# Two transformer layers on one core: part by part reordering of the sequence stage, of the y turn and of the weight preparation

## The chip, the cores and the metric

One core of a Trainium2 chip runs the whole program in one launch. The metric is the device time in microseconds (us); three runs of the kernel before took 2637.14, 2634.07 and 2632.92 us, median 2634.07.

## The reference

Input x is 2048 x 576 (S x D) in fp32. Two layers, each a Fourier mixing and an MLP:

```
A(x) = Cr @ (x @ dr.T) - Ci @ (x @ di.T)         # 2048 x 2048 and 576 x 576 DFT matrices
B(x) = gelu(layernorm(x) @ w1 + b1) @ w2 + b2    # 576 -> 4608 -> 576
for layer in range(2):
    x = x + A(layernorm(x))
    x = x + B(layernorm(x))                       # both layers use the same weights
```

## The kernel before, in words

**Products of parts.** TensorE gets each fp32 operand as two rounded parts: ACT copies it to a high part (fp32r), VectorE subtracts to make the low part. A product is three matmul passes, (high, high), (high, low), (low, high), in PASSES as (left, right). The large products go by a scheme with seven block products in place of eight (numbered 1 to 7, in the order ORDER); it needs sums and differences of blocks on both sides, which VectorE and POOL make, and its results are combined in PSUM and SBUF.

**Sequence stage** (class Sequence). S x S times S x 576, from x that has been normalized, in NT = 16 row tiles of output. The right operand is 8 pairs of x tiles, Z[p], each with 7 blocks in two parts: three plain blocks (rows 0 to 2 of Z), b12 aside, and four sums (rows 3 to 6). While the pairs come in, the first PLAIN = 2 tiles are made by eight plain products (`first_mms(p)`, 48 matmuls per pair, banks 0 to 7), so that TensorE has work. A generator, `fill`, emits for every pair: loads, statistics (`norm_stats`), mean and scale by a pow on POOL, `normalize` on ACT, high parts (`high_left`, `high_z`), low parts (`low_left`, `low_z`), and the sums (`right_sums` on VectorE and POOL, `high_sums`, `low_sums`). `run` emits first_mms(p) as soon as pair p's emission is done. Then come 14 tiles of seven products of 24 matmuls (`mms`), each with left blocks loaded (`load_c`), summed (`sums`), cut in parts (`high` three steps ahead, `low` two steps ahead) and results collected (`post`). BANK gives each product its bank; products that share one are accumulated or follow each other. In layer 1 the first pairs are prepared inside the MLP before (early = True).

**Weight preparation.** w1 is cut in parts once, in layer 0: `weights()` is a generator of 4 + 1 + 2 x 126 steps (18 column pairs q of 7 blocks), driven by `pump()`. Of each two steps one emits the low part of block n (VectorE), the sum that follows it (POOL) and the high part of block n + 1 (ACT), the other the store of block n to DRAM and perhaps a load for the next q. Three stage slots hold the parts: block n + 3 reuses block n's. `made[0]` is q + 1 once pair q's seven blocks are stored. In the sequence stage of layer 0 two pumps follow each product but product 2 (L759 to 761). In the first MLP `advance` pumps at the places in BEHIND, twelve per group from group 1 on, and `load_w` has `while made[0] <= q: pump()` ahead of a load of pair q's parts. Five slots hold loaded w1 parts there, so the first block of q + 1 is asked for before the fourth product of q.

**Hidden stage and MLP.** `hidden` multiplies with the 576 x 576 matrices, normalizes, and turns blocks of 128 tokens (index j) by TensorE into y, seven rows of blocks with two parts. `turn_y(3)` does so for the last block, between the first products of the MLP (`inner(0, 0)`, first half of the tokens, columns 0 to 255 of y; the second half follows). `parts(2, ...)` makes the parts of block 2. In `mlp`, `inner(q)` makes seven products into banks 0 to 3 or 4 to 7 and their gelu, `outer(g, i, side)` multiplies by w2. The list `due` holds the steps that make w2's parts in the first MLP (`make(g)`), by place within the group. Each engine executes in the order in which its instructions are emitted.

Of the kernel before, what the change touches and what calls it, by code (L numbers as in the profile page):

```python
# [15 lines left out]
P = 128  # L16
# [17 lines left out]
ORDER = (1, 6, 2, 5, 7, 3, 4)  # L34
BANK = {1: 0, 2: 0, 6: 1, 5: 2, 3: 2, 7: 3, 4: 3}
# [10 lines left out]
PASSES = ((0, 0), (0, 1), (1, 0))  # L46

# [111 lines left out]
def spectral_mixer(ctx: ExitStack, tc: tile.TileContext, x, dh, c0, cs, w1, b1, w2, b2, out):  # L159
# [102 lines left out]
    def weights():  # L262
# [5 lines left out]
                 (7, a21, None), (6, a11, None), (3, a12, None))  # L268
# [25 lines left out]
        def keep(n):  # L294
# [3 lines left out]
            if k in (2, 4, 5, 6):  # L298
                load(q + 1, (2, 4, 5, 6).index(k))
# [28 lines left out]
    class Sequence:  # L328
        def __init__(self, src, early):
# [4 lines left out]
            self.normal, self.begun, self.xs, self.before = set(), {}, [], self.prepare()  # L334
            self.pieces = self.fill()
# [33 lines left out]
        def fill(self):  # L369
# [32 lines left out]
            else:  # L402
# [14 lines left out]
                self.high_parts(0)  # L417
                yield
            for p in range(NP):
# [22 lines left out]
                if p == 0 and not self.early:  # L442
                    self.half_stats(1)
                    self.low_z(0)
                    self.norm_stats(1)
                    self.low_left(0)
                    yield
# [39 lines left out]
            self.low(*self.steps[0], True)  # L487
            self.high(*self.steps[1])
            self.right_sums(NP - 1)
            self.high(*self.steps[2])  # L490
            self.high_sums(NP - 1)
            self.low(*self.steps[1])
# [44 lines left out]
        def norm_stats(self, p):  # L537
            if p not in self.mv:
# [3 lines left out]
                self.mv[p] = stats_of_pair(st, mv, p == 0 and not self.early, p > 2, p == 1 and not self.early)  # L542

        def normalize(self, p):
            for h in range(2):
                at = slice(2 * h, 2 * h + 2)
                if p == 0 and not self.early:
                    v, mv = self.x[p][:, at], self.mv[p][:, h]
                    nc.vector.tensor_scalar(v, v, mv[:, 0:1], mv[:, 3:4], op0=OP.subtract, op1=OP.mult)
                    continue  # L550
                if p == 1 and not self.early:
                    shift(self.mv[p][:, h])
# [27 lines left out]
        def low_left(self, p):  # L580
            c = self.left(p)
            sub(nc.vector, c[:, 1], self.lv[p], c[:, 0].bitcast(F32))
# [21 lines left out]
        def first_mms(self, p):  # L604
            c, z, b = self.left(p), self.Z[p](7, 2, DH), self.b12[p](2, DH)
            right = {(1, 1): z[:, 0], (2, 2): z[:, 1], (2, 1): z[:, 2], (1, 2): b}
            cells = [(t, i, j, k) for t in range(PLAIN) for i in (1, 2) for j in (1, 2) for k in (1, 2)]
            steps = [(*cell, n) for n in range(3) for cell in cells]
            if p == NP - 1:
                steps = [(*cell, n) for cell in cells for n in range(3)]  # L610
            for t, i, j, k, n in steps:
                o, (u, w) = banks[4 * (1 - t) + 2 * (i - 1) + j - 1][:, :DH], PASSES[n]
# [56 lines left out]
        def low(self, t, i, sums=False):  # L669
            v = self.cells[t, i](2, NP, P)  # L670
            sub(nc.vector, v[:, 1], self.source(t, i), v[:, 0].bitcast(F32))
            if sums:
                self.sums(t)
# [798 lines left out]
```

## Time and profile before

| what | value |
|---|---|
| median of three runs | 2634.07 us |
| profiled execution, own time | 2634.11 us |
| its span, first to last instruction | 2632.3 us |
| TensorE matmul (PE), weight loads (PEld) busy | 2617.2 us, 2466.4 us |
| VectorE (DVE), ScalarE (ACT), GpSimd (POOL) busy | 1834.1, 1118.3, 796.7 us |
| granted TensorE clock | 1.000 |

Busy times are unions over the span. A matmul's end is modelled, and matmuls overlap. SP issues most transfers. The helpers at L196 (add), L199 (subtract), L202 (split) and L209 (matmul) record many operations under one line. The sequence stage of layer 0 takes the first 380 us or so, its first MLP lies at about 450 to 850 us, layer 1's sequence stage begins near 1319 us.

### The profile page before, as it was taken

How to read it: one execution, taken by the hardware profiler on the slowest of the kernel's cores; microseconds unless marked ns; L12 is line 12 of the kernel's file. 1: busy time of each engine (PE TensorE's matmuls, PEld its weight loads, DVE VectorE, ACT ScalarE, POOL GpSimd, SP SyncE). 2: the span in 40 equal slices, each digit the busy share in tenths (PEclk: the TensorE clock that was granted, in tenths of full speed). 3: DMA queues.
4: the chain of work that ended last, by engine and by line, in shares of the span. 5: the costliest groups of instructions: out<-in, count | busy, mean ns of one | idle time of the engine just before them, and what ended most of it. 6: DMA issues, size and time to landing. Idle time of an engine off the chain costs nothing. (4 is left out here: it accounts for less than half of the span.)

```text
span 2632.3 us, 44772 instructions
## 1 busy us (share of the span) xinstructions
PE 2617.2 (99%) x17252; PEld 2466.4 (94%) x17252; DVE 1834.1 (70%) x2574; ACT 1118.3 (42%) x1815; POOL 796.7 (30%) x644
## 2 busy tenths in 40 slices
PE   9999999999999999999999999999999999999999
PEld 9999999899999989998999999999999999899998
DVE  8999987878777665556687776576555557655555
ACT  6555555555453443333354333353333325433332
POOL 6333433534444332222251000132222233322222
PEclk9999999999999999999999999999999999999999
DMA  5687786788788666677554333746666685666664
GB/s 184 226 273 241 244 259 215 262 276 286 275 286 299 184 194 195 195 222 212 170 177 132 124 123 124 210 153 192 195 195 195 195 274 157 200 195 194 194 195 156
DMA packets 223238, 544.91 MB, mean 207 GB/s; under 512 B 23712, under 2 KB 74912, under 8 KB 222880
## 3 DMA queue, kind: packets, MB, share of 16 engines
q1 hardware_dynamic: 209632, 511.94, 61.9%
q10 hardware_dynamic: 13392, 30.09, 3.0%
q8 instruction: 137, 2.24, 0.3%
q14 instruction: 77, 0.63, 0.1%
HBM read 429.87 MB, written 114.72 MB: 207 GB/s over the span
## 5 line engine op out<-in xcount | busy, mean ns | idle before, releaser
L209 PE MATMUL bank<-R 128*128 128x288 f32 (+2 forms) x16972 | 2587.4, 315 | 9.0 <-DVE R L199 3.8
L209 PEld LDWEIGHTS bank<-R 128*128 128x128 f32 x16972 | 2435.4, 189 | 157.0 <-DVE R L199 7.0
L196 DVE TENSOR_TENSOR A<-bank,A 128x576 f32<-128x576 f32 (+3 forms) x810 | 567.5, 708 | 520.2 <-PE bank L209 464.2
L199 POOL TENSOR_TENSOR R<-A,R 128x512 fp32r<-128x512 f32 (+1 forms) x290 | 376.0, 1305 | 909.6 <-ACT R L1261 548.7
L199 DVE TENSOR_TENSOR R<-A,R 128x1024 fp32r<-128x1024 f32 (+9 forms) x535 | 530.4, 1017 | 43.8 <-ACT R L667 12.5
L1261 ACT ACTIVATE R<-A 128x512 fp32r<-128x512 f32 x288 | 177.5, 630 | 355.7 <-DVE A L199 222.1
L196 POOL TENSOR_TENSOR A<-A 128x576 f32<-128x576 f32 (+2 forms) x102 | 156.2, 1536 | 539.5 <-ACT A L708 344.2
L1200 ACT ACTIVATE bank<-bank,b1t 128x512 f32<-128x512 f32 (+1 forms) x224 | 144.9, 647 | 360.9 <-DVE bank L196 235.8
L199 POOL TENSOR_TENSOR A<-A 128x288 f32<-128x288 f32 (+3 forms) x152 | 192.6, 1271 | 200.1 <-DVE R L199 95.3
L196 DVE TENSOR_TENSOR bank<-bank,A 128x512 f32<-128x512 f32 (+1 forms) x228 | 152.2, 669 | 143.5 <-PE bank L209 142.6
L667 ACT ACTIVATE R<-A 128x1024 fp32r<-128x1024 f32 x196 | 206.1, 1053 | 103.4 <-PE bank L209 60.2
L199 DVE TENSOR_TENSOR A<-A 128x1024 f32<-128x1024 f32 (+3 forms) x166 | 164.5, 996 | 6.2
L199 DVE TENSOR_TENSOR R<-bank,R 128x512 fp32r<-128x512 f32 x232 | 156.2, 676 | 4.3 <-ACT R L1261 3.7
L1261 ACT ACTIVATE R<-bank 128x512 fp32r<-128x512 f32 x216 | 121.1, 595 | 32.5 <-PE bank L209 32.5
L199 DVE TENSOR_TENSOR A<-bank,A 128x512 f32<-128x512 f32 x144 | 98.1, 681 | 0.4
L1227 ACT ACTIVATE A<-bank 128x512 f32<-128x512 f32 (+1 forms) x76 | 43.7, 575 | 120.2 <-PE bank L209 120.2
L282 ACT ACTIVATE R<-A 128x256 fp32r<-128x256 f32 x126 | 51.9, 412 | 64.0 <-DMA w_parts<-R 23.1
L1200 ACT ACTIVATE A<-bank,b1t 128x512 f32<-128x512 f32 (+1 forms) x76 | 50.5, 665 | 66.6 <-DVE bank L196 66.5
L230 POOL TENSOR_TENSOR moments<-moments,power 128x1 f32<-128x1 f32 x32 | 26.7, 834 | 129.8 <-DVE moments L232 112.0
L283 ACT ACTIVATE R<-A,power,middle 128x128 fp32r<-128x128 f32 x126 | 60.6, 481 | 0.0
L256 ACT ACTIVATE A<-A,moments 128x576 f32<-128x576 f32 x58 | 49.0, 866 | 23.5 <-POOL moments L252 13.6
L1135 ACT ACTIVATE R<-A 128x576 fp32r<-128x576 f32 x63 | 42.2, 676 | 15.8 <-DVE A L199 7.2
(65 smaller groups left out, 609.6 us busy)
## 6 DMA issues: line engine op xcount, KB each, us to landing
R<-w_parts SPq DMA_DIRECT2D x504, 320.0 KB, 3.4
R<-w_parts SPq DMA_DIRECT2D x189, 576.0 KB, 3.7
A<-in_cs SPq DMA_DIRECT2D x112, 512.0 KB, 4.5
w_parts<-R SPq DMA_DIRECT2D x63, 576.0 KB, 5.1
w_parts<-R ACTq DMA_DIRECT2D x81, 320.0 KB, 3.8
uv_mid<-A SPq DMA_DIRECT2D x28, 576.0 KB, 5.4
w_parts<-R SPq DMA_DIRECT2D x45, 320.0 KB, 4.5
A<-in_w SPq DMA_DIRECT2D x72, 192.0 KB, 4.9
```

What stands on the lines that cost most here:

```text
L196: engine.tensor_tensor(dst, a, b, op=op)
L199: engine.tensor_tensor(dst, a, b, op=OP.subtract)
L209: nc.tensor.matmul(o, a, b, start=start, stop=stop, skip_group_check=True)
L230: nc.gpsimd.tensor_tensor(mv[:, 3:4], mv[:, 2:3], power[:, 0:1], op=OP.pow)
L256: nc.scalar.activation(dst, src, AF.Identity, bias=mv[:, 4:5], scale=mv[:, 3:4])
L282: nc.scalar.activation(t[:, 1:4:2], src[:, 0:3:2], AF.Copy)
L283: nc.scalar.activation(t[:, 2], src[:, 1], AF.Identity, bias=power[:, 2:3], scale=middle)
L667: nc.scalar.activation(self.cells[t, i](2, NP, P)[:, 0], self.source(t, i), AF.Copy)
L1135: nc.scalar.activation(got2[g, i](2, 2, DH)[:, :, 0], src, AF.Copy)
L1200: nc.scalar.activation(dst, src, AF.Gelu_apprx_tanh, bias=bias(f))
L1227: nc.scalar.activation(up, o, AF.Copy)
L1261: nc.scalar.activation(H[q, k](2, TC)[:, 0], src, AF.Copy)
```

## The change

It has these parts; the core of the diff follows.

- First pairs, layer 0: `first_parts` makes the parts of pair 0 in halves on ACT; the left low parts of pair 0 come in two halves around the statistics of pair 1, and the right low parts after them. Pair 7 gets its mean and scale by VectorE and ACT (`quick`), no longer by POOL.
- `first_mms` passes in the order (high, high), (low, high), (high, low), and with other orders of cells; in the last pair all (high, high) first.
- The first seven-product tile runs in the order FIRST; product 2 has a bank of its own there, and is added by VectorE. The emission at the end of `fill` is ordered for it.
- No pump in the first seven products, and none after the third product of a tile; the preparation's blocks 6 and 7 are exchanged, with the loads that follow.
- `turn_y`: the seven short transposes go to other banks, four and three apart; the low parts of block 2 come after the whole turn.
- MLP: places of w2's steps in the first and the last group; one difference on POOL for the first q.

```diff
+FIRST = (1, 2, 6, 5, 7, 3, 4)
+LEFT_FIRST = ((0, 0), (1, 0), (0, 1))
 # weights()
-                 (7, a21, None), (6, a11, None), (3, a12, None))
+                 (6, a11, None), (7, a21, None), (3, a12, None))
-                load(q + 1, (2, 4, 5, 6).index(k))
+                load(q + 1, {2: 0, 4: 2, 5: 1, 6: 3}[k])
 # Sequence
+            self.quick = (NP - 1,) if early else (1, NP - 1)
-                self.high_parts(0)
+                self.first_parts()
                 if p == 0 and not self.early:
+                    self.low_left(0, 0)
                     self.half_stats(1)
+                    self.norm_stats(1)
+                    self.low_left(0, 1)
                     self.low_z(0)
-                    self.norm_stats(1)
-                    self.low_left(0)
-            self.low(*self.steps[0], True)
+            self.right_sums(NP - 1)
             self.high(*self.steps[1])
-            self.right_sums(NP - 1)
+            self.low(*self.steps[0])
+            self.low(*self.steps[1])
+            self.sums(PLAIN)
+            sub(nc.vector, self.block(PLAIN, 0), self.tmp(NP, P), self.block(PLAIN, 0))
+            self.high_sums(NP - 1)
             self.high(*self.steps[2])
-            self.high_sums(NP - 1)
-            self.low(*self.steps[1])
             self.low_sums(NP - 1)
...
-                self.mv[p] = stats_of_pair(st, mv, p == 0 and not self.early, p > 2, p == 1 and not self.early)
+                self.mv[p] = stats_of_pair(st, mv, p == 0 and not self.early, 2 < p < NP - 1, p in self.quick)
+        def first_parts(self):
+            x, z, mv = self.x[0], self.Z[0](7, 2, DH), self.mv[0]
+            self.parts[0], self.b12[0] = self.own.take(), self.b12s[0]
+            left = self.left(0)
+            for h in range(2):
+                v = x[:, 2 * h:2 * h + 2]
+                nc.vector.tensor_scalar(v, v, mv[:, h, 0:1], mv[:, h, 3:4], op0=OP.subtract, op1=OP.mult)
+            nc.scalar.activation(left[:, 0, 0:4], self.lv[0][:, 0:4], AF.Copy)
+            nc.scalar.activation(z[:, 0, 0], x[:, 1], AF.Copy)
+            nc.scalar.activation(self.b12[0](2, DH)[:, 0], x[:, 0], AF.Copy)
+            nc.scalar.activation(z[:, 1:3, 0], x[:, 2:4], AF.Copy)
+            nc.scalar.activation(left[:, 0, 4:8], self.lv[0][:, 4:8], AF.Copy)
 # first_mms
+            if p == 0:
+                cells = [(t, i, j, k) for t in range(PLAIN) for k in (1, 2) for j in (1, 2) for i in (1, 2)]
+            elif p < NP - 1:
+                cells = [(t, i, j, k) for j in (1, 2) for t in range(PLAIN) for i in (1, 2) for k in (1, 2)]
             steps = [(*cell, n) for n in range(3) for cell in cells]
             if p == NP - 1:
-                steps = [(*cell, n) for cell in cells for n in range(3)]
+                steps = [(*cell, 0) for cell in cells] + [(*cell, n) for cell in cells for n in (1, 2)]
 # begin_loads, low, mms, post
-            self.steps = [(t, i) for t in range(PLAIN, NT) for i in ORDER]
+            self.steps = [(t, i) for t in range(PLAIN, NT) for i in (ORDER if t > PLAIN else FIRST)]
-            if i == 2:
+            if i == (2 if t > PLAIN else 6):
                 sub(nc.vector, self.block(t, 1), self.block(t, 1), self.block(t, 0))
+        def bank(self, t, i):
+            return banks[4 - 4 * (t % 2) + (3 if t == PLAIN and i == 2 else BANK[i])][:, :DH]
+            elif i == 2 and t == PLAIN:
+                add(nc.vector, uv[:, 0, 1], b, p1)
 # run
-                if i != 2:
+                if n % 7 != 2 and n >= 7:
                     pump()
                     pump()
 # turn_y, hidden
-            o = space()
-            for i0 in (0, 4):
+            late = space()[:, 1:2, :3 * P]
+            for i0, o in ((0, pp[0][:, :, TC // 2:]), (4, late)):
...
-        for n in (4, 2, 0):
+        for n in (4, 1, 1):
             next(mlp)
             for m in range(n):
-                if n == 4 and m == 2:
-                    parts(2, slice(0, 4), slice(3, 7), high=False, engine=nc.gpsimd)
-                    t8s.give(t8.pop(2))
                 next(y_steps)
+        parts(2, slice(0, 4), slice(3, 7), high=False, engine=nc.gpsimd)
+        t8s.give(t8.pop(2))
 # mlp
-                return (list(zip((22, 23, 26), one + five[:1])),
-                        list(zip((6, 6, 8, 8, 10, 10, 12, 12, 14, 14, 16), five[1:] + six + three + seven + two + four)))
+                return (list(zip((22, 25), one)),
+                        list(zip((6, 7, 7, 8, 8, 10, 10, 12, 12, 14, 14, 16), five + six + three + seven + two + four)))
-                    sub(nc.vector if n < 4 or first and q == 0 and n < 6 else nc.gpsimd, h[:, 1], src, h[:, 0].bitcast(F32))
+                    sub(nc.vector if n < 4 or first and q == 0 and n == 5 else nc.gpsimd, h[:, 1], src, h[:, 0].bitcast(F32))
-                due.extend((n, step) for n, (_, step) in zip((3, 4, 5, 6, 9, 10), soon + late[:4]))
+                due.extend((n, step) for n, (_, step) in zip((3, 4, 7, 8, 11, 12), soon + late[:4]))
```

## Rows read from the trace of the kernel before

**Rows 1.** Page, first part: busy us (share of the span) xinstructions.
```profile
PE 2617.2 (99%) x17252; PEld 2466.4 (94%) x17252; DVE 1834.1 (70%) x2574; ACT 1118.3 (42%) x1815; POOL 796.7 (30%) x644
```
**Rows 2.** Waits of the weight loads, whole span: us in total, times, longest us.
```profile
PEld bank L209 <- DVE R L199: 7.0, 13, 1.5
```
**Rows 3.** Timeline, first pairs: start, us, engine, line, operation [idle before <-releaser].
```profile
8.91 1.43 DVE L199 TENSOR_TENSOR R<-A,R 128x864 fp32r<-128x864 f32 x2 [0.43 <-ACT R L569]
...
11.60 1.68 POOL L247 TENSOR_TENSOR moments<-moments,power 128x2 f32<-128x2 f32 x1 [5.20 <-DVE moments L249]
...
16.79 38.32 PEld L209 LDWEIGHTS bank<-R 128*128 128x128 f32 x289 [1.41 <-ACT R L569]
```
**Rows 4.** Timeline, pair 3, last pair and first tile of layer 0.
```profile
28.38 0.93 ACT L569 ACTIVATE R<-A 128x864 fp32r<-128x864 f32 x1
...
55.76 13.00 PEld L209 LDWEIGHTS bank<-R 128*128 128x128 f32 x97 [0.65 <-DVE R L199]
...
69.33 12.50 PEld L209 LDWEIGHTS bank<-R 128*128 128x128 f32 x94 [0.58 <-DVE R L199]
```
**Rows 5.** Windows: busy us (x) of PE, PEld, DVE, ACT, POOL; clock, DMA.
```profile
16.80:55.30 38.50, 38.50 (x289) 38.27 (x289) 36.71 (x61) 30.00 (x38) 33.35 (x35) 1.00 0.51 174
```
**Rows 6.** Waits of the weight loads, 80 to 145 us.
```profile
PEld bank L209 <- DVE R L199: 3.3, 5, 1.5
PEld bank L209 <- ACT A L708: 0.7, 1, 0.7
```
**Rows 7.** Timeline, ACT in the preparation.
```profile
110.99 0.42 ACT L282 ACTIVATE R<-A 128x256 fp32r<-128x256 f32 x1 [6.69 <-DMA A<-in_w]
```
**Rows 8.** Waits of the weight loads, 1352 to 1400 us (layer 1).
```profile
PEld bank L209 <- DVE R L199: 1.4, 3, 0.6
```
**Rows 9.** Waits of the weight loads, 457 to 470 us.
```profile
PEld bank L209 <- DVE bank L196: 1.0, 1, 1.0
PEld bank L209 <- ACT A L1227: 0.9, 1, 0.9
```
**Rows 10.** Waits of the weight loads, 820 to 831 us.
```profile
PEld bank L209 <- ACT R L1261: 0.8, 1, 0.8
```
**Rows 11.** Timeline, the last turn of y.
```profile
2226.93 0.82 PEld L1011 LDWEIGHTS bank<-ident,A 128*96 128x96 f32 x7 [0.54 <-POOL A L199]
...
2227.33 1.45 DVE L199 TENSOR_TENSOR R<-A,R 128x1024 fp32r<-128x1024 f32 x1
...
2227.78 2.30 POOL L196 TENSOR_TENSOR A<-A 128x576 f32<-128x576 f32 x1
...
2229.64 0.75 DVE L196 TENSOR_TENSOR bank<-bank,A 128x256 f32<-128x256 f32 x2
...
2230.88 7.26 PEld L209 LDWEIGHTS bank<-R 128*128 128x128 f32 x49 [0.59 <-ACT A L1227]
```
**Rows 12.** Line L282, 0 to 400 us: count, ns, first and last start.
```profile
L282 ACT ACTIVATE R<-A x83: 396/418/421, 79.7 to 383.2; 128x256 fp32r<-128x256 f32 x83
```
**Rows 13.** Timeline, groups 7 and 8 of the first MLP.
```profile
769.18 0.41 ACT L282 ACTIVATE R<-A 128x256 fp32r<-128x256 f32 x1
...
791.50 0.79 SPq L297 DMA_DIRECT2D w_parts<-R  x2
...
792.59 19.50 PEld L209 LDWEIGHTS bank<-R 128*128 128x128 f32 x126 [0.38 <-DVE A L196]
```
**Rows 14.** DMA issues at 768.90 and 773.84: KB, us to landing.
```profile
w_parts<-R SPq DMA_DIRECT2D x1, 320.0 KB, 2.7
...
w_parts<-R SPq DMA_DIRECT2D x1, 320.0 KB, 7.0
```
**Rows 15.** Windows at the start, columns as in rows 5.
```profile
1.00:3.00 2.00, 1.66 (x8) 1.66 (x9) 0.00 (x0) 1.21 (x2) 0.55 (x5) 1.00 0.60 168
...
5.00:7.00 2.00, 2.00 (x21) 2.00 (x20) 1.05 (x6) 0.00 (x0) 0.72 (x1) 1.00 0.97 328
```
**Rows 16.** Window in group 7 of the first MLP, columns as rows 5.
```profile
764.00:776.00 12.00, 12.00 (x57) 10.02 (x56) 7.21 (x12) 7.16 (x15) 3.88 (x4) 1.00 0.72 224
```

More of the change, by code (lines that the diff above doesn't have):

```diff
@@ L546, in normalize @@
                 at = slice(2 * h, 2 * h + 2)
[L547 to L551, printed above, removed]
+                if p in self.quick:
                     shift(self.mv[p][:, h])
@@ L578, in low_z, with low_left @@
             self.ready = p + 1
-        def low_left(self, p):
-            c = self.left(p)
-            sub(nc.vector, c[:, 1], self.lv[p], c[:, 0].bitcast(F32))
+        def low_left(self, p, t=None):
+            c, at = self.left(p), slice(0, 8) if t is None else slice(4 * t, 4 * t + 4)
+            sub(nc.vector, c[:, 1, at], self.lv[p][:, at], c[:, 0, at].bitcast(F32))
         def left(self, p):
@@ L667, in high, with low @@
             nc.scalar.activation(self.cells[t, i](2, NP, P)[:, 0], self.source(t, i), AF.Copy)
-        def low(self, t, i, sums=False):
+        def low(self, t, i):
             v = self.cells[t, i](2, NP, P)
             sub(nc.vector, v[:, 1], self.source(t, i), v[:, 0].bitcast(F32))
-            if sums:
-                self.sums(t)
-            if i == 1:
+            if i == 1 and t > PLAIN:
                 sub(nc.vector, self.block(t, 0), self.tmp(NP, P), self.block(t, 0))
-            if i == 2:
+            if i == (2 if t > PLAIN else 6):
                 sub(nc.vector, self.block(t, 1), self.block(t, 1), self.block(t, 0))
@@ L680, in low @@
                 self.give(t, {7: 2, 3: 1, 4: 3}[i])
+        def bank(self, t, i):
+            return banks[4 - 4 * (t % 2) + (3 if t == PLAIN and i == 2 else BANK[i])][:, :DH]
         def mms(self, t, i):
-            c, b = self.cells[t, i](2, NP, P), banks[4 - 4 * (t % 2) + BANK[i]]
+            c, b = self.cells[t, i](2, NP, P), self.bank(t, i)
+            alone = t == PLAIN and i in (1, 2)
             for p in range(NP):
@@ L686, in mms @@
                 for n, (u, w) in enumerate(PASSES):
-                    mm(b[:, :DH], c[:, u, p], z[:, RIGHT[i], w], i in OPENS and p == 0 and n == 0,
-                       i in CLOSES and p == NP - 1 and n == 2)
+                    mm(b, c[:, u, p], z[:, RIGHT[i], w], (i in OPENS or alone) and p == 0 and n == 0,
+                       (i in CLOSES or alone) and p == NP - 1 and n == 2)
             self.own.give(self.cells.pop((t, i)))
@@ L692, in post @@
         def post(self, t, i):
-            b = banks[4 - 4 * (t % 2) + BANK[i]][:, :DH]
+            b = self.bank(t, i)
             if i == 2:
@@ L739, in run @@
                     self.low(*steps[n + 2])
-                if i == 2 and t + 1 < NT:
+                if n % 7 == 2 and t + 1 < NT:
                     self.sums(t + 1)
@@ L745, in run @@
                 self.mms(t, i)
-                self.post(t, i)
                 if n == 1:
@@ L749, in run @@
                     hidden.reserve()
+                self.post(t, i)
+                if n == 1:
                     self.first_post(1, outs[1])
@@ L1005, in turn_y @@
                 yield
-            o = space()
-            for i0 in (0, 4):
-                ov = o[:, i0 // 4].rearrange("p (i t) -> p i t", t=P)
+            late = space()[:, 1:2, :3 * P]
+            for i0, o in ((0, pp[0][:, :, TC // 2:]), (4, late)):
+                ov = o.rearrange("p a (i t) -> p a i t", t=P)
                 ni = min(4, 7 - i0)
                 for i in range(ni):
-                    nc.tensor.transpose(ov[:96, i], es(7, 96)[:, blocks[i0 + i] - 1], ident)
-                nc.scalar.activation(y[:96, i0:i0 + ni, 2, at], ov[:96, :ni], AF.Copy)
+                    nc.tensor.transpose(ov[:96, i // 2, i % 2] if i0 == 0 else ov[:96, 0, i],
+                                        es(7, 96)[:, blocks[i0 + i] - 1], ident)
+                to = y[:96, i0:i0 + ni, 2, at]
+                nc.scalar.activation(to.rearrange("p (a i) t -> p a i t", a=2) if i0 == 0 else to[:, None],
+                                     ov[:96], AF.Copy)
                 yield
```

2 lines of the change are left out of this document (1 added, 1 removed).

## The prediction

> **What bounds the kernel now.** I read the page's busy table first. TensorE shows work in 2617 of 2632 us [rows 1], so no other engine can be sped up into a gain: an edit pays only where it takes away a stop of TensorE. Matmuls overlap, and the matmul row shows less of a stop than it costs (of the one at 16.79 us less than the 1.41 that the weight loads show [rows 3]), so second I read what the weight loads waited for, of which VectorE's low parts are the largest entry with 7.0 us [rows 2], and take the loads' idle time as the price of a stop. The 15 us in which no matmul ran are 0.6% of the span. Third, the timeline around each. I work against the profiled execution, 2634.11 us with a span of 2632.3; the 1.8 us around the span I leave as they are, and the median of the runs shown is 2634.07, the same. A timing of this kernel can tell about 0.2%, 5.3 us, from no change: faster means under 2628.8, slower over 2639.3.
>
> **The first pairs of layer 0.** TensorE finishes pair 0 and stands 1.41 us until ACT has the high parts of pair 1. That chain hangs on the pow on POOL at 11.60, which waited until VectorE had done the right low parts of pair 0 (8.91, 1.43 us, itself after 0.43 us of idling) [rows 3]. The change puts the statistics of pair 1 ahead of these low parts and only half a left block (some 0.6 us) before them, in the time that was idle and the start of the 1.43. I let the chain move up by about 1.4: pair 1 is ready near 15.35, TensorE arrives at 15.2. That takes 1.3 off. TensorE doesn't starve meanwhile: the new pass order reads the left low parts second and the right low parts third, 32 matmuls after its start (32 x 0.13 = 4.2 us, about 13.0 us), and I have VectorE done with them at about 12.1. Not all of it is kept. VectorE works 36.7 of the next 38.5 us [rows 5] and gains only its two idle waits, 0.43 and 0.35, about 0.8. Pair 3's high parts end at 29.31 [rows 4] where TensorE, 96 matmuls after 16.79, came at about 29.5: they had 0.2 to spare. TensorE early by 1.3 against parts early by 0.8 + 0.2 gives back 0.3. The last pair's stop of 0.65 [rows 4] goes: 16 matmuls (2.1 us) now need only high parts and cover the low ones, and the pair's mean and scale go by VectorE and ACT instead of three POOL steps (0.33 us of VectorE more, hidden by that same 2.1). Sum: -1.3 + 0.3 - 0.65 = **-1.65**. Making the first pair by halves gains at most the 0.18 us that its first load waited; the warm-up transposes end just before it, so I count nothing.
>
> **The first seven-product tile.** It opens with products 1 and 2, whose right operands need no sums: 48 matmuls (6.3 us) before the summed rows of the last pair are read. The stop at 69.33 (0.58, on VectorE's low parts [rows 4]) loses its cause. The weight preparation stays out of this tile (n >= 7), and with it the ACT work that held the 0.7 stop on L708 [rows 6]. VectorE has nearly a tile's 22 us of work there, and ACT waits for its transpose before two copies that product 4 needs, so I leave 0.4: **-0.85**.
>
> **Tiles 3 to 5.** Five stops on VectorE sum to 3.3 us [rows 6]: it carries the preparation from the first product on and runs late. With 12 steps fewer there, and products 6 and 7 of the preparation exchanged so that block a11 is fetched two steps (one product, 3.15 us) earlier, ACT's 6.69 us wait for that fetch [rows 7] shrinks; the stop of 1.5 us came right behind it. POOL's sum now waits for the other block, and VectorE stays nearly full: 0.7 left, **-2.6**. Layer 1 has no preparation; its three stops of 1.4 us [rows 8] are the last pair and the first tile again: **-1.0**.
>
> **The opening of the MLP and its end.** Two stops of 0.9 and 1.0 us [rows 9] stand where the first w2 parts are made among the first products. The change puts four of these steps two slots later and one difference on POOL, off VectorE (0.68 us): **-1.3**, with 0.6 kept for the steps that now fall into the next product. The stop near 827 us (0.8 [rows 10]) has one part of the last w2 group beside it, moved by two slots; I keep 0.2: **-0.6**.
>
> **The turn of the last y block, four times.** In the rows of the last one, VectorE does two splits, then the low parts of block 2 (2227.33, 1.45 us), two more splits, and the sums of products 3 and 4 at 2229.64; ACT's gelu and copy come after those, and TensorE waits 0.59 at 2230.88 for product 2 of the second half; before that the seven transposes had waited 0.54 for a bank and the es rows [rows 11]. The change gives these transposes other banks, and puts the 1.45 us last on VectorE. But those low parts cover columns of y that the second half reads: ORDER is 1, 6, 2, and product 6 takes row 5, one of rows 3 to 6. So product 6 becomes the waiting one. VectorE's work is the same and ends as before at 2230.39; then 6 matmuls of product 6 (0.72) and the restart (0.2) put product 2 at about 2231.3 instead of 2230.88. +0.45 each, 1.8; 0.2 off since the first one runs into the stops of rows 9: **+1.6**. The two ends are -1.1 each (both waits go and nothing comes) and +1.45 each (the whole operation is exposed). POOL's addition of 2.30 us [rows 11] runs beside that stretch, and the 1.45 was taken beside it too, so I charge nothing more. By the Trainium skill (SBUF — State Buffer, "Who interferes with whom") a VectorE instruction with two SBUF inputs and a POOL instruction that reads SBUF shut each other out for a whole instruction; by that rule the moved operation, which now starts some 1.4 us after the addition, could be held by what is left of it, 0.9 us each time, 3.6 in all and 2638.3; the trace has the two overlapping from 2227.78 on without such a delay of the 1.45, so I leave this within the forecast's own range.
>
> **The preparation that was left out comes due.** This is the largest term. The weights need 257 steps. Before, 168 were made in the first sequence stage: 83 of the 126 high parts stand there [rows 12], as 4 + 2 x 82 steps give. Now n >= 7 leaves 13 tiles x 12 = 156. BEHIND is not changed: 12 steps per group from group 1. load_w may not load w1 of product pair q before all of q is made (19 + 14q steps), and it asks for the next q before the fourth product of each. At group 7, second half, q = 16 wants 243; there were 168 + 72 + 9 = 249, now 237, so 6 steps are forced in one go. At group 8, first half, q = 17 wants 257; there were 255 (the forced last store stands right behind its forerunner at 791.50, as this count has it [rows 13]), now 249, so 8 are forced. In such a burst each new high part needs one of three stage slots whose store has landed, ACT and VectorE are in order, and behind the burst stands VectorE's sum of product 5, which product 3 on TensorE needs. First burst: the slot's store goes out at 768.90 and lands 2.7 us later [rows 14], 771.6; a high part of 0.8 us (two ACT instructions, the first at 769.18 [rows 13]), a low part of 0.55 and the sum's 0.7 give 773.7 instead of the end of product 7 at 771.8. 1.9, and 0.8 for the next high part, whose store goes out 1.8 us later and holds VectorE once more. Second: the later of the two stores that it waits for leaves near 792.0, so 794.7, and high, low and sum make 796.7 against 792.59 [rows 13]: 4.1, and 0.2 after it. **+7.0**. From below it is nothing, if the two engines' idle time there absorbs the waits; from above, with a store that takes 7.0 us as one at 773.84 did [rows 14], 773.7 becomes 778 and 796.7 becomes 801: about 15.
>
> **Sum.** -1.65 - 0.85 - 2.6 - 1.0 - 1.3 - 0.6 = -8.0; +1.6 + 7.0 = +8.6. 2634.1 + 0.6 = **2634.7 us**.
>
> **Rivals.** (A) The bursts cost nothing: 2634.7 - 7.0 = 2627.7. For it: VectorE and ACT work 7.2 of the 12 us around the first one [rows 16]; against: both are in order, so idle time behind a wait is no use. (B) Slower: the bursts' stores meet the w2 traffic and land after 7 us, as [rows 14] show for one right there; then the bursts take 15 and the time is 2642.7. It decides from a landing of about 5 us on. (C) The y turns gain: product 6's parts are there in time, -1.1 each instead of +0.45: 2634.7 - 6.0 = 2628.7. Against it: from the operation's 2227.33 to the sums' end at 2230.39 VectorE has hardly a gap [rows 11]. (D) The first tile doesn't do what it says: product 6, third now, still waits for the last pair's sums, which the new order puts behind two more low parts; without the 0.85 and half of layer 1's gain, 2636.1. (E) TensorE loses its clock: it is granted 1.00 throughout and never stops over 1.5 us; the second burst would stop it 4.1. At the start, where it came from rest, it issued 8 transposes in two microseconds against 21 in a later two [rows 15], until 4.97 us; a fall to that pace (1.2 of 2.4 GHz) for as long costs 1.8: 2636.5. The Trainium skill (TensorE: Matmul & The Clock Gate, "HAM oscillation — how this bites in real kernels") names waits of this kind between matmuls as what lowers the clock; no run here shows one.
>
> **Chances.** The forecast 0.41 (own range 2631 to 2639), A 0.21, B 0.15, C 0.11, D 0.07, E 0.05. Faster: most of A, half of C and a little of the forecast, 0.27. Slower: most of B and a little of forecast, D and E, 0.18. Same 0.55. The range runs from A to short of B, 2627.0 to 2641.5.
>
> **What would show it.** After: no stop at pair 1 and a short one at pair 3; none over 0.4 in the first tile; two stops of TensorE on VectorE's L196 near 764 and 785 us (8 us earlier), with ACT waiting for w_parts just before; at each y turn a wait on L199 ahead of the second matmul of product 6. Without those two stops near the end of the first MLP the step with the bursts is wrong, and so is the forecast.

## The result, and the profile after

The changed kernel takes 2639.03 us (median of 22 runs, 2637.59 to 2640.91) where the one before takes 2634.34 beside it: 1.0015 times as long, interval 1.0009 to 1.0022. That is 4 to 5 us slower, inside the stated range (2627.0 to 2641.5) and inside the 0.2% that the prediction counts as no change; 2634.7 had been forecast. The profiled execution has a span of 2637.6 us against 2632.3.

Helper lines moved by two: L198 adds, L201 subtracts, L204 splits, L211 is the matmul. The busy row that answers to [rows 1]:

```profile
PE 2617.1 (99%) x17252; PEld 2466.4 (94%) x17252; DVE 1838.0 (70%) x2580; ACT 1120.9 (42%) x1819; POOL 789.4 (30%) x639
```

TensorE's busy time is the same to 0.1 us, so the 5.3 us of span show as time without work. The weight loads' waits over the whole span (us in total, times, longest) answer to [rows 2]:

```profile
PEld bank L211 <- DVE A L198: 7.5, 6, 4.2
PEld bank L211 <- DVE R L201: 5.8, 9, 1.0
PEld bank L1037 <- ACT bank L1228: 4.6, 4, 1.2
...
PEld bank L211 <- POOL R L201: 1.1, 1, 1.1
```

The entry of VectorE's additions was this one before:

```profile
PEld bank L209 <- DVE A L196: 1.4, 6, 0.4
```

Low parts (L201) went from 7.0 to 5.8 us, and VectorE's additions from 1.4 to 7.5, of which the two bursts have 6.1. Two entries are new: four short transposes of the y turn behind ACT's gelu, and one wait of products on POOL. The first pairs and the first tile in the timeline after, to hold against [rows 3, 4]:

```profile
10.48 1.15 POOL L249 TENSOR_TENSOR moments<-moments,power 128x2 f32<-128x2 f32 x1 [3.93 <-DVE moments L251]
...
15.14 6.38 PEld L211 LDWEIGHTS bank<-R 128*128 128x128 f32 x48 [0.35 <-ACT R L586]
22.22 1.89 PEld L211 LDWEIGHTS bank<-R 128*128 128x128 f32 x14 [0.71 <-ACT R L586]
...
67.87 4.26 PEld L211 LDWEIGHTS bank<-R 128*128 128x128 f32 x32 [0.97 <-DVE R L201]
```

The pow started 1.1 us earlier, pair 1's stop fell from 1.41 to 0.35, pair 2 (48 matmuls further on) got one of 0.71, pair 3 has none, and the first tile has one stop, at product 6. The second burst, after:

```profile
788.75 4.87 SPq L299 DMA_DIRECT2D w_parts<-R  x5
...
790.99 0.42 ACT L284 ACTIVATE R<-A 128x256 fp32r<-128x256 f32 x1 [1.36 <-DMA w_parts<-R]
...
791.83 0.56 DVE L201 TENSOR_TENSOR R<-A,R 128x384 fp32r<-128x384 f32 x1 [1.09 <-ACT R L285]
...
793.18 0.68 DVE L198 TENSOR_TENSOR A<-bank,A 128x512 f32<-128x512 f32 x1
...
793.92 3.06 PEld L211 LDWEIGHTS bank<-R 128*128 128x128 f32 x8 [4.17 <-DVE A L198]
```

Five stores go out in a row; a high part waits for one to land, a low part for the high part, and VectorE's sum of product 5 stands behind them; TensorE waits 4.17 us for it. The windows around it (length, busy us and count of PE, PEld, DVE, ACT, POOL, then the granted clock, DMA share, GB/s):

```profile
785.00:789.70 4.70, 4.70 (x22) 3.86 (x21) 3.74 (x4) 3.61 (x8) 3.16 (x3) 1.00 0.64 236
789.70:793.90 4.20, 0.47 (x3) 0.04 (x1) 2.78 (x5) 1.60 (x4) 2.16 (x2) 0.87 0.73 283
793.90:799.70 5.80, 5.78 (x14) 4.53 (x15) 1.94 (x3) 1.35 (x2) 2.79 (x2) 0.50 1.01 329
799.70:805.00 5.30, 5.30 (x41) 5.26 (x40) 3.18 (x5) 2.84 (x5) 0.00 (x0) 1.00 0.82 302
```

After the stop the granted clock was 0.50 (1.2 of 2.4 GHz) and 14 matmuls ran in 5.8 us. The last y turn, after [rows 11]:

```profile
2232.08 0.47 ACT L1228 ACTIVATE bank<-bank,b1t 128x256 f32<-128x256 f32 x1
2232.61 0.17 PEld L1037 LDWEIGHTS bank<-ident,A 128*96 128x96 f32 x2 [1.15 <-ACT bank L1228]
...
2234.24 1.22 DVE L201 TENSOR_TENSOR R<-A,R 128x1024 fp32r<-128x1024 f32 x1
...
2235.51 2.57 PEld L211 LDWEIGHTS bank<-R 128*128 128x128 f32 x21 [0.58 <-DVE R L201]
```

The third short transpose waits for a gelu; product 6 waits for the low parts of block 2.

The price of a stop is, from here on, the excess of the spacing between matmul starts over the median spacing for their number of columns. Counting those over 0.05 us, they sum to 26.1 us before and 32.3 after, of which the table has 18.7 and 25.0:

| place | before | after | change | forecast |
|---|---|---|---|---|
| first pairs, layer 0 | 2.47 | 1.11 | -1.4 | -1.65 |
| first seven-product tile | 1.41 | 1.01 | -0.4 | -0.85 |
| tiles 3 to 5 | 3.90 | 0.25 | -3.65 | -2.6 |
| layer 1, first pairs and tile | 1.53 | 1.13 | -0.4 | -1.0 |
| MLP opening, 459 to 482 us | 1.54 | 3.09 | +1.55 | -1.3 |
| near 830 us | 1.00 | 1.42 | +0.4 | -0.6 |
| y turns, four | 6.62 | 8.57 | +1.95 | +1.6 |
| two bursts, with the clock | 0.22 | 8.37 | +8.15 | +7.0 |

For the y turns the time over the same matmuls is the safer measure, as some spacings behind a stop are shorter than the median. Over 89 spacings of each turn, from 29 matmuls ahead of its seven short transposes on, the four take 47.99 us before and 49.55 after: +1.6.

### The profile page after: what moved, and what is told of

It reads as the page before. It is cut to its first block, busy times and chain, and to the rows that moved or that the text cites. A ratio compares the mean times of both kernels' runs of the same rounds, so it can differ in the third digit from the quotient of the medians.

```text
span 2637.6 us, 44763 instructions
## 1 busy us (share of the span) xinstructions
PE 2617.1 (99%) x17252; PEld 2466.4 (94%) x17252; DVE 1838.0 (70%) x2580; ACT 1120.9 (42%) x1819; POOL 789.4 (30%) x639
## 5 line engine op out<-in xcount | busy, mean ns | idle before, releaser
L211 PE MATMUL bank<-R 128*128 128x288 f32 (+2 forms) x16972 | 2589.3, 314 | 12.2 <-DVE A L198 5.5
L211 PEld LDWEIGHTS bank<-R 128*128 128x128 f32 x16972 | 2435.9, 189 | 160.7 <-DVE A L198 7.5
L198 DVE TENSOR_TENSOR A<-bank,A 128x576 f32<-128x576 f32 (+3 forms) x812 | 568.5, 708 | 518.6 <-PE bank L211 470.3
L201 POOL TENSOR_TENSOR R<-A,R 128x512 fp32r<-128x512 f32 (+1 forms) x291 | 377.6, 1306 | 925.8 <-ACT R L1289 569.3
L201 DVE TENSOR_TENSOR R<-A,R 128x1024 fp32r<-128x1024 f32 (+9 forms) x535 | 534.5, 1023 | 44.2 <-ACT R L688 13.7
L198 POOL TENSOR_TENSOR A<-A 128x576 f32<-128x576 f32 (+2 forms) x102 | 148.3, 1458 | 569.9 <-ACT A L733 333.5
L198 DVE TENSOR_TENSOR bank<-bank,A 128x512 f32<-128x512 f32 (+1 forms) x228 | 152.8, 670 | 146.9 <-PE bank L211 145.9
L201 POOL TENSOR_TENSOR A<-A 128x288 f32<-128x288 f32 (+3 forms) x152 | 195.4, 1288 | 163.9 <-DVE R L201 77.3
L201 DVE TENSOR_TENSOR A<-A 128x1024 f32<-128x1024 f32 (+3 forms) x166 | 164.1, 993 | 6.2
L201 DVE TENSOR_TENSOR R<-bank,R 128x512 fp32r<-128x512 f32 x232 | 156.1, 677 | 5.9 <-ACT R L1289 5.3
L201 DVE TENSOR_TENSOR A<-bank,A 128x512 f32<-128x512 f32 x144 | 98.3, 682 | 0.4
L198 DVE TENSOR_TENSOR A<-A 128x1024 f32<-128x1024 f32 x28 | 36.3, 1296 | 19.0 <-DMA A<-in_cs 15.3
```

Of the source, the lines that this page charges most:

```text
L198: engine.tensor_tensor(dst, a, b, op=op)
L201: engine.tensor_tensor(dst, a, b, op=OP.subtract)
L211: nc.tensor.matmul(o, a, b, start=start, stop=stop, skip_group_check=True)
```

## The experiments

**The bursts.** Two places more per group (run e1) let groups 1 to 6 make the twelve missing steps:

```diff
-BEHIND = (0, 2, 2, 4, 5, 6, 15, 17, 17, 19, 21, 21)
+BEHIND = (0, 2, 2, 4, 5, 6, 11, 15, 17, 17, 19, 21, 21, 26)
```

> The changed kernel with two more places per group in BEHIND (11 and 26), so groups 1 to 6 make the 12 steps that the sequence stage no longer makes; all else as changed. Theory (the forced bursts cost time, by their stops and by the clock that fell after the second): the stops at 769.0 (1.75 us) and from 793.9 on (6.6 us with the slower clock) go, the granted clock stays 1.00, the 12 steps hide beside the matmuls of groups 1 to 6: 2639.0 - 8.4 = 2630.6 us. Rival 1 (what is forced late is only work moved; spread out, it stops TensorE elsewhere for as long): about 2638. Rival 2 (the stop goes but the fall of the clock was chance and not tied to it): 2633, with the clock still down somewhere.

2631.65 us, 0.9988 of before (0.9979 to 0.9997). No weight load waits between 750 and 800 us, and the window shows the clock at 1.00:

```profile
750.00:800.00 50.00, 50.00 (x307) 45.88 (x306) 39.44 (x59) 23.08 (x43) 20.30 (x15) 1.00 0.78 282
```

The theory holds (-7.4 timed, -8.4 expected): without the bursts nothing is left of the loss. Next, the preparation back among the first seven products, in the changed kernel, and kept out of them in the kernel before:

```diff
 # e2_first_tile_pumps, from the changed kernel
-                if n % 7 != 2 and n >= 7:
+                if n % 7 != 2:
 # b1_shift_alone, from the kernel before
-                if i != 2:
+                if i != 2 and n >= 7:
```

> The changed kernel with the preparation put back among the first seven products, all other edits kept. The two bursts go, as all 168 steps are made in the sequence stage again (-8.4 us). Theory (the gain in tiles 1 to 5 came from leaving the preparation out): the stops of 0.6 to 1.5 us on VectorE and ACT in the first five tiles return, of the 5.2 us that they had cost before (5.2 now gone but for 1.0) some 3.5 to 4: 2634 to 2635 us. Rival (the new order of products, the order of emission and the exchange of blocks 6 and 7 made that gain alone): no stop over 0.5 comes back there, 2630.6 us.

> The kernel before with one edit alone: no preparation in the first seven products. Theory (the stops in tiles 1 to 5 came from VectorE's load by the preparation, and the late preparation is the price): of the 3.9 us of stops between 90 and 141 us some 3 go, the two stops near 771 and 796 us (1.8 and 6.6 with the clock at half) come, and the stop of 1.1 near 480: 2634.4 - 3 + 9.5 = 2640.9 us. Rival 1 (the new order of the first tile and the exchange of the preparation's blocks 6 and 7 are needed for that gain): the stops between 90 and 141 stay, 2643.9. Rival 2 (the bursts come from the edits of the MLP and not from the shift): no burst, 2631.5.

e2 took 2634.95 us (1.0000, 0.9991 to 1.0009): no burst, and the waits of weight loads from 60 to 145 us are largely back (5.0 us in the kernel before, 1.2 in the changed one):

```profile
PEld bank L211 <- DVE R L201: 2.6, 4, 1.1
PEld bank L211 <- ACT A L733: 0.9, 1, 0.9
```

b1 took 2640.18 us (1.0024, 1.0015 to 1.0033). Its bursts between 760 and 804 us, and the same view for 60 to 145 us:

```profile
PEld bank L209 <- DVE A L196: 6.5, 2, 4.6
```
```profile
PEld bank L209 <- DVE R L199: 1.9, 3, 1.1
```

Both theories hold in the main: the shift alone brings the bursts, and with it the waits of 3.3 us on low parts and 0.7 on ACT from 80 us on [rows 6] become 1.3; the view has 0.6 more at 69.7 us. The exchange of blocks 6 and 7 and the order FIRST do little without the shift, but not nothing: from the start of the first seven-product tile to that of the fifth TensorE takes 94.5 us before, 93.2 in e2, 91.0 in b1 and 90.2 after, by the starts of the matmuls. So the shift alone gives 3.5 of the 4.3 us, the other edits alone 1.3.

**The y turn.** It was put back as before, `turn_y` and the place of `parts(2, ...)` with it; then, in the changed kernel, two other places were tried for the first four short transposes:

```diff
 # e3_old_turn
-        for n in (4, 1, 1):
+        for n in (4, 2, 0):
...
 # y1_other_bank
-            for i0, o in ((0, pp[0][:, :, TC // 2:]), (4, late)):
+            for i0, o in ((0, bank[:, 0:4:3, TC // 2:]), (4, late)):
 # y2_own_bank
+            for i0, o in ((0, pp[2][:, 0:1]), (4, late)):
```

> The changed kernel with the turn of the last y block as it was (seven short transposes in one place, the low parts of block 2 between the splits). Theory (the turn costs more than before since the short transposes wait 1.15 us for ACT's gelu and product 6 waits 0.6 us for the low parts, where before two waits of 0.65 stood): four times 0.45 us back, 2637.2 us; in the trace no stop of 1.15 at the short transposes, stops of about 0.55 to 0.65 twice at each turn. Rival (the turn is bound by VectorE's and ACT's work there, whatever the order): within 0.5 us of 2639.0, with the stops of a turn summing as now (some 2.0 us).

> The changed kernel with the first four short transposes of the y turn in the second halves of banks 0 and 3 in place of banks 0 and 1; the order of all instructions is the same. Theory (the third transpose waits 1.15 us since ACT's gelu works in the first half of bank 1, but VectorE is nearly as late): the 1.15 us stop goes, VectorE comes to the low parts of block 2 only 0.3 us earlier, and the wait of product 6 grows from 0.6 to about 1.45 us: 0.3 us less per turn, 2639.0 - 1.2 = 2637.8 us. Rival 1 (the stop was the whole delay): product 6's wait stays 0.6, 1.15 less per turn, 2634.4 us. Rival 2 (it isn't the bank: the transposes wait for ACT whatever bank they take): the wait for the gelu stays at 1.15 us, 2639.0.

> The changed kernel with the first four short transposes in bank 4, which holds no product of the MLP then (the first splits of the turn had it), the last three in bank 5 as before. Theory (an instruction on TensorE waits for any other engine's work in the same bank, in either half; with that out of the way VectorE is the bound): the 1.15 us in front of the third short transpose go but for some 0.3, the wait of product 6 grows from 0.63 to about 1.2 us as VectorE comes to the low parts of block 2 only 0.3 us earlier: 0.3 us less per turn, 2637.8 us. Rival 1 (the bank was the whole delay): product 6 waits 0.6 us still, 0.85 less per turn, 2635.6 us. Rival 2 (the clock falls as with banks 0 and 3): a longer turn, over 2640.

e3: 2637.46 us (1.0010, 1.0001 to 1.0019); over the same matmuls the four turns take 47.66 us in place of 49.55, 0.47 less for each, as expected. y1 was a miss on all sides: 2648.71 us (1.0050, 1.0036 to 1.0064). The gelu's wait went, but product 4, in the first half of bank 3, now waited for ACT's copy of the transposes out of the second halves of banks 0 and 3, and ACT's copy for VectorE:

```profile
2240.49 0.59 ACT L1040 ACTIVATE R<-bank 96x512 fp32r<-96x512 f32 x1 [1.12 <-DVE bank L198]
...
2241.13 0.89 PEld L211 LDWEIGHTS bank<-R 128*128 128x128 f32 x7 [2.65 <-ACT R L1040]
```
```profile
2238.40:2241.10 2.70, 0.34 (x4) 0.09 (x1) 1.97 (x5) 1.58 (x5) 2.39 (x2) 1.00 0.00 0
2241.10:2246.00 4.90, 4.87 (x28) 4.85 (x29) 1.68 (x3) 1.21 (x3) 0.00 (x0) 0.65 0.10 18
```

The clock fell behind this stop, in all four turns. Whether a bank as a whole or the range from bank 0 to bank 3 makes product 4 wait, this run can't tell. y2, in a bank of its own, is the cleaner test: 2638.38 us (1.0015, 1.0006 to 1.0025), in time no different from the change; the rows decide:

```profile
2230.87 0.39 PEld L1037 LDWEIGHTS bank<-ident,A 128*96 128x96 f32 x4 [0.53 <-POOL A L201]
...
2232.86 1.37 DVE L201 TENSOR_TENSOR R<-A,R 128x1024 fp32r<-128x1024 f32 x1
...
2234.28 2.82 PEld L211 LDWEIGHTS bank<-R 128*128 128x128 f32 x23 [0.87 <-DVE R L201]
```

The wait of 1.15 became 0.53 (on the es rows, as before the change), and product 6's grew from 0.58 to 0.87: a turn takes 0.30 less than with the change (48.36 us for the four). Of the 0.62 taken off in front, about half is given back at product 6, so VectorE's low parts are the bound there. The total is the theory's, with other shares (it had 0.3 left in front and 1.2 at product 6); rival 1's 0.85 per turn is out.

**The opening of the MLP and the place near 830 us.** First the opening alone as before, then everything in the MLP and the y turn as before with the two places more, then the same with the preparation begun a product later:

```diff
 # e4_old_opening
-                    sub(nc.vector if n < 4 or first and q == 0 and n == 5 else nc.gpsimd, h[:, 1], src, h[:, 0].bitcast(F32))
+                    sub(nc.vector if n < 4 or first and q == 0 and n < 6 else nc.gpsimd, h[:, 1], src, h[:, 0].bitcast(F32))
-                due.extend((n, step) for n, (_, step) in zip((3, 4, 7, 8, 11, 12), soon + late[:4]))
+                due.extend((n, step) for n, (_, step) in zip((3, 4, 5, 6, 9, 10), soon + late[:4]))
 # c1_combined: e1 + e3 + e4, and in make()
-                return (list(zip((22, 25), one)),
+                return (list(zip((22, 23, 26), one + five[:1])),
...
 # c2_phase: c1, and
-                if n % 7 != 2 and n >= 7:
+                if n % 7 != 2 and n >= 8:
```

> The changed kernel with the places of the first w2 parts (3, 4, 5, 6, 9, 10) and VectorE for the n = 4 difference as they were. Theory (that edit made the opening worse, as POOL makes the difference in 2.5 us where VectorE took 0.7, and ACT's copy and TensorE's outer product wait for it): the stops between 455 and 485 us, 3.1 us now, come down to the 1.5 of before: 2637.5 us. Rival 1 (the y turn in front of it made it worse, not this edit): unchanged, 2639. Rival 2 (the edit helped at 468 and the stop at 481 comes from elsewhere): slower than 2639.5.

> The changed kernel with two more places in BEHIND (11 and 26), and the y turn, the places of the first w2 parts with their difference on VectorE, and the places in the last group as before: what is left of the change are its edits to the sequence stage and the late preparation. Theory (the terms add up): 2631.65 for the two places alone, less 1.7 for four turns, 0.4 at the opening, 0.35 near 830 us: 2629.2 us; stops of 0.65 and 0.64 at each turn, 0.74 and 0.83 near 455 to 462, one of some 1.0 near 480 (POOL makes preparation sums ahead of the differences that the outer products need), 0.8 near 826. Rival (the edits hide one another's cost, so that undoing them together gives less): 2631 or above.

> The kernel c1_combined with the preparation starting after the first eight products of the sequence stage in place of seven: 154 steps there, 14 fewer than before the change, which is one whole round of seven blocks, so that in each group of the MLP the same blocks stand at the same places as before the change. Theory (the stop of 1.1 us near 480 comes from the round being shifted by one block, which puts two sums on POOL ahead of the differences that the outer products wait for): that stop goes, no forced burst appears (2 more places per group make 154 + 98 + 6 = 258 of 257 steps by the time when the last pair is asked for), 2628.1 us. Rival (the stop comes from the opening's own steps or from the w2 parts): it stays, 2629.2 us.

e4 missed: 2638.95 us (1.0017, 1.0008 to 1.0026). The two stops near 460 came down from 1.96 to 1.57, as the theory says, but the one near 481 stayed at 1.0. c1 took 2628.04 us (0.9975, 0.9966 to 0.9985), 1.2 less than the sum expected; its stops near 822 us are 0.78 and 0.21, as before the change. c2 took 2628.75 (0.9977, 0.9968 to 0.9986), the same time, but the stop near 481 is gone. POOL ahead of it in c1, then in c2:

```profile
473.68 1.02 POOL L198 TENSOR_TENSOR A<-A 128x384 f32<-128x384 f32 x1 [8.84 <-DVE R L201]
474.65 2.54 POOL L201 TENSOR_TENSOR R<-A,R 128x512 fp32r<-128x512 f32 x2
477.15 1.34 POOL L201 TENSOR_TENSOR A<-A 128x384 f32<-128x384 f32 x1
```
```profile
477.76 1.02 POOL L198 TENSOR_TENSOR A<-A 128x384 f32<-128x384 f32 x1 [2.81 <-DVE R L201]
```

c1 has two preparation sums (128x384) there, c2 one: with 156 steps made, the round of seven blocks is shifted against the groups, and the second sum stands ahead of the differences of H that the outer product waits for. The other runs agree: b1, the shift alone, has the stop too (1.1 at 484 us), and e2, with 168 steps made, has none there. In its profile c2 pays elsewhere: one stop of 1.73 at 135.7 us, on ACT.

**Pair 1.**

```diff
 # p1_stats_late
-                    self.norm_stats(1)
                     self.low_left(0, 1)
                     self.low_z(0)
+                    self.norm_stats(1)
```

> The changed kernel with the statistics of pair 1 once more behind the low parts of pair 0 on VectorE; the new pass order and the halves stay. Theory (pair 1's chain hangs on the pow, which waits for VectorE): the pow on POOL starts some 2 us later than 10.48, the high parts of pair 1 come some 2 us late, and TensorE stops about 2 us at pair 1, where the changed kernel stops 0.4; the 0.7 at pair 3 goes. Some 1 to 1.3 us slower in all, 2640.2, read from the stops. Rival (the halves and the new pass order moved the chain, not the place of the statistics): the stop at pair 1 stays near 0.4 us.

One run, 2643.26 us. The pow and the stop, and the window behind it:

```profile
12.23 1.21 POOL L249 TENSOR_TENSOR moments<-moments,power 128x2 f32<-128x2 f32 x1 [5.84 <-DVE moments L251]
...
16.94 7.13 PEld L211 LDWEIGHTS bank<-R 128*128 128x128 f32 x42 [2.25 <-ACT R L586]
```
```profile
16.90:22.00 5.10, 5.05 (x26) 5.06 (x27) 5.04 (x10) 5.07 (x7) 2.37 (x4) 0.67 0.98 354
```

The pow is 1.75 us later and the stop is 2.25: the place of the statistics did it. The clock fell here too, which was not expected, and with it the stop's price is 3.8.

**The clock.**

```diff
 # d1_doses: e1, and in inner(), layer 1 alone
                 elif i == 5:
-                    add(nc.vector, tp, o, up)
+                    for _ in range(1 + (0 if first else DOSE.get((half, ends, q), 0))):
+                        add(nc.vector, tp, o, up)
```

> The kernel e1_more_pumps (no forced burst, no stop over 1.6 us after the start) with one addition of the MLP on VectorE, the sum of product 5, made several times over (the same result each time) in some products of layer 1, so that TensorE stops for chosen times. Extra copies in the first MLP half: 4, 5, 6, 7, 8, 10, 13 at q = 3, 5, 7, 9, 11, 13, 15; in the second half 13, 10, 8, 7, 6, 5 at the same places up to 13. At 0.7 us a copy, with some 0.6 us of room, the stops are about 2.2, 2.9, 3.6, 4.3, 5.0, 6.4 and 8.5 us. Theory (a stop of TensorE alone, if long enough, brings the granted clock down to half afterwards, as after the 4.2 us stop of the changed kernel, and the slower matmuls cost some 2.4 us more): short doses leave the clock at 1.00 and cost their stop alone; from some length between 1.9 and 4.2 us on it falls to 0.5 for some 7 us and 2 to 3 us are added; the same length does the same in both halves. Rival (the clock fell there for another reason, as the load of the other engines and queues): no fall at any dose, or falls that don't go with length.

Five of the thirteen stops, then the 10 us behind each (busy us and count of PE, granted clock, DMA share, GB/s):

```profile
1808.58 44.81 PEld L213 LDWEIGHTS bank<-R 128*128 128x128 f32 x266 [2.56 <-DVE A L200]
1856.67 44.82 PEld L213 LDWEIGHTS bank<-R 128*128 128x128 f32 x266 [3.28 <-DVE A L200]
1905.49 46.32 PEld L213 LDWEIGHTS bank<-R 128*128 128x128 f32 x266 [4.01 <-DVE A L200]
...
2537.25 46.36 PEld L213 LDWEIGHTS bank<-R 128*128 128x128 f32 x266 [4.01 <-DVE A L200]
2586.89 13.29 PEld L213 LDWEIGHTS bank<-R 128*128 128x128 f32 x69 [3.28 <-DVE A L200]
```
```profile
1808.60:1818.60 10.00, 10.00 (x65) 1.00 0.47 141
1856.70:1866.70 10.00, 10.00 (x65) 1.00 0.41 127
1905.50:1915.50 10.00, 10.00 (x53) 0.83 0.29 81
...
2537.30:2547.30 10.00, 10.00 (x53) 0.83 0.31 87
2586.90:2596.90 10.00, 10.00 (x44) 0.70 0.24 67
```

The stop of 2.56 left the clock at 1.00. Those of 3.28 did so once and lost it once. All ten of 4.01 to 9.08 lost it. By the spacing of the matmuls behind the stop itself, a loss cost 1.6 to 2.9 us, and not more for a longer stop (1.7 behind 9.08); where the clock stayed, 0.1. So a stop alone can lower the clock, as the theory has it; that the same length does the same in both halves is refuted at 3.28, and y1 and p1 lost it behind 2.65 and 2.25. What else decides is open.

**The first tile.**

```diff
 # f1_high_early, from c1; at the end of pair 7's high parts, no longer behind right_sums(7)
                     self.high(PLAIN, 1)
+                    self.high(*self.steps[1])
```

> The kernel c1_combined with the high part of product 2's left block (first seven-product tile, both layers) ahead of the four copies out of PSUM on ACT, where it stood behind them; nothing else moves. Theory (the stop of 0.93 us at product 6 of the first tile, 0.98 in layer 1, is the end of an unbroken chain on VectorE: low parts, sums, low parts of the last pair, low part of product 6's left block; the chain's one gap is 0.49 and 0.47 us of waiting for that high part): both stops fall by the gap, to some 0.45 to 0.5 us, and 0.9 us go: 2627.1 us, where c1_combined took 2628.0. Rival 1 (product 6 waits for POOL's sums of the last pair, as rival D of the prediction has it, not for the chain on VectorE): the stops stay. Rival 2 (the copies, now 1 us later, hold the bank of the first tile's first product): a new stop of up to 1 us at the tile's start.

2628.28 us (0.9976, 0.9965 to 0.9986), as c1: the theory missed. In layer 0 the stop is 0.32, but TensorE came to the first pairs 1.3 us later there, without the stops at pairs 1 and 2, and VectorE's chain, as long as in c1, began 0.4 earlier; in layer 1 the stop is 0.98 as before. VectorE's low parts of the first two left blocks and POOL's sums beside them in layer 1, in c1 and then in f1:

```profile
1367.34 3.40 POOL L201 TENSOR_TENSOR A<-A 128x288 f32<-128x288 f32 x2 [3.53 <-ACT A L643]
...
1368.80 1.28 DVE L201 TENSOR_TENSOR R<-A,R 128x1024 fp32r<-128x1024 f32 x1 [0.47 <-ACT R L688]
```
```profile
1367.87 2.97 DVE L201 TENSOR_TENSOR R<-A,R 128x1024 fp32r<-128x1024 f32 x2
...
1368.10 3.40 POOL L201 TENSOR_TENSOR A<-A 128x288 f32<-128x288 f32 x2 [3.53 <-DVE A L201]
...
1377.56 1.50 PEld L211 LDWEIGHTS bank<-R 128*128 128x128 f32 x11 [0.94 <-DVE R L201]
```

The gap went and the operation behind it took longer: 2.97 us for the two, where 1.22 + 0.47 + 1.28 are 2.97. The second low part ends 2.74 us after POOL's start in both (1370.08 in c1, 1370.84 in f1), 1.08 after the first of POOL's two subtractions has ended (1369.00 and 1369.76, taken from the single records). So VectorE waits for POOL there. By the Trainium skill (SBUF — State Buffer, "Who interferes with whom"), a VectorE instruction with two SBUF inputs and a POOL instruction that reads SBUF exclude each other for a whole instruction; this trace agrees, as the end of VectorE's instruction keeps its 1.08 us from the end of POOL's whenever it starts.

## Why the prediction was right, and which steps of it failed

The time was inside a range of 14.5 us, 4.3 above the forecast, by a sum in which steps that failed were partly made up by others that gave more; that part is luck. The two largest misses are the MLP opening (+2.85) and the fall of the clock (+2.7), the largest in their favour tiles 3 to 5 (-1.05) and the end of the bursts (-1.0). The burst, the largest term, was right in its mechanism.

- **The bursts (+7.0)** came as counted: two stops, 1.91 and 4.17 us of waiting for 1.9 and 4.1 forecast. e1 and b1 show that the pump condition alone makes them. At the first, ACT shows no wait for w_parts, though that was named as a sign: the store issued at 764.67 landed after 2.2 us, at 766.9, just as ACT came free for the next high part. TensorE stood from 767.1 and from 789.7, not from 764 and 785, as less had been gained ahead of them. What was mis-sized is the end: the 1.0 us after the bursts did not come, and the clock did fall. Rival E was priced at 1.8 us and given 0.05; it happened on top of the forecast, 2.7 us by the spacing after 793.92. The Trainium skill (TensorE: Matmul & The Clock Gate, "HAM oscillation — how this bites in real kernels") names waits between matmuls as its cause; these traces agree now, with 0.50 behind the 4.17. Rivals A and B are out: the bursts cost 8.15, neither nothing nor 15, and the five stores of the second landed in 2.2 to 2.5 us, not in 7.
- **Tiles 3 to 5 (-2.6)** gave 3.65, mostly by the shift: b1, the shift alone, gives 2.6 of it.
- **First pairs (-1.65)** gave 1.4, by the step named (p1). The part given back is 0.7 at pair 2, not 0.3 at pair 3: the "0.2 to spare" was counted for pair 3 alone, and ACT's first high parts of pair 2 ended at 22.17 us, later than the 21.55 of before.
- **The first tile (-0.85) and layer 1 (-1.0)** gave 0.4 each. "The stop at 69.33 loses its cause" failed: product 6 came too early for VectorE, much as rival D has it, and a stop of 1.0 stands there instead. f1 shows that POOL's subtractions hold the chain on VectorE ahead of it; that the stop would go without them was not tried.
- **The MLP opening (-1.3)** failed in sign, +1.55. The four steps and the difference on POOL cost 0.4 (e4), and the profile has ACT's copy, for which TensorE waits 1.58, behind POOL (lines below); the other 1.1 is a term that I had not seen, the shifted round of the preparation (c2). "One difference on POOL, off VectorE" counted VectorE's 0.68 and not the 1.3 us that POOL takes for it, nor who waits for POOL.

```profile
465.94 1.28 POOL L201 TENSOR_TENSOR R<-A,R 128x512 fp32r<-128x512 f32 x1
...
467.25 0.60 ACT L1255 ACTIVATE A<-bank 128x512 f32<-128x512 f32 x1 [3.97 <-POOL R L201]
```

- **Near 830 us (-0.6)**: +0.4. Moving the part brought two later stops; c1, with the old places, has the old ones.
- **The y turns (+1.6)** came out at +1.6, but more than half by another road: I had let the transposes' wait go, and it doubled; product 6's wait came where it was named, only 0.58 long, since TensorE had already stood at the transposes (y2, with 0.53 there, has 0.87) and the low parts took 1.22 and not 1.45. That the total fits is luck. Rival C is out. I had also read the exclusion wrongly in [rows 11]: POOL's addition took 2.30 there and takes 1.42 after, so POOL waited for VectorE's 1.45; and the 1.45 itself, 1.22 without POOL beside it, ended at 2228.78, 1.08 us behind this subtraction on POOL, the same distance as in f1:

```profile
2226.43 1.27 POOL L199 TENSOR_TENSOR R<-A,R 32x512 fp32r<-32x512 f32 x1
```

## What to carry to other kernels

Work that is moved out of a full stage has to be paid for at its due date: count what the consumers force, and raise the rate in between (here two places per group, 7.4 us). An operation moved to another engine costs its time on that engine and what stands behind it there, and a periodic background task has a phase that any change in its count shifts against the loops it runs beside. In this kernel a stop of TensorE of 2.25 us or more should be priced with a possible loss of clock, 1.6 to 2.9 us more. The sequence-stage edits with the late preparation spread out and the rest as before (c1) beat both kernels: 2628.04 us, 6.6 us under the one before (2634.60 beside it).

## What the runs showed of the hardware that was not expected

- A loss of the granted clock cost as much behind a stop of 9.08 us (1.7) as behind one of 4.01 (1.7), and was seen behind stops as short as 2.25.
- TensorE's transposes into one half of a PSUM bank stood behind ACT's gelu on the other half for 1.15 us (y2, in a bank of their own, doesn't have this wait); by the profile a semaphore of the program holds them.
- VectorE's low part of 1.22 us took 1.83 us when POOL's subtraction, begun earlier, still ran (f1); the profile shows this as a longer instruction and not as idle time, so closing the gap ahead of it gained nothing.
